# Linear attention and a multiplicative FFN on one core: attention matmuls at full height, another phi, a chunk per batch, and a new order

## The chip, the core and the metric

The kernel runs on one NeuronCore of a Trainium2 chip. Five engines work side by side, each through its own list of instructions in order, and wait for one another by semaphores: TensorE (PE, matmuls, with its weight loads as PEld), VectorE (DVE), ScalarE (ACT), GpSimd (POOL) and SyncE (SP, which only issues DMAs here). Sixteen DMA engines move data; SP, POOL and ACT put work on their queues. PE writes to PSUM (8 banks of 512 fp32 columns), the others read it from there; POOL has no work on PSUM in this kernel.

The metric is the device time of one execution in microseconds. The kernel before took 261.28 us (median of 3 runs, 260.99 to 262.19).

## The reference

```python
def phi(x):                                       # elu(x) + 1
    return np.where(x > 0, x, np.exp(x) - 1.0) + 1.0
q_p, k_p = phi(q), phi(k)                         # q, k, v: 8 batches, 8 heads, 576 tokens, 64
kv  = np.einsum('bhsd,bhse->bhde', k_p, v)        # 64 x 64 for each head
z   = np.sum(k_p, axis=2)
num = np.einsum('bhsd,bhde->bhse', q_p, kv)
den = np.einsum('bhsd,bhd->bhs', q_p, z)[..., None] + 1e-06
x   = (num / den).transpose(0, 2, 1, 3).reshape(4608, 512)
a, b = x @ w1, x @ w2                             # 512 -> 1024
out = ((a * b) @ w3) @ w_out                      # 1024 -> 1024 -> 512
```

All inputs and the output are fp32. Both kernels compute with bf16 operands and fp32 sums, and multiply w3 and w_out once, into one 1024 x 512 matrix wf, so that the last two products become one.

## The kernel before

**Tiles.** The 576 tokens of a batch are four tiles of 128 ("J": token 4p + j is in tile j at partition p) and a rest of 64 ("R"). Two batches share one R tile, one in each half of the partitions. So 36 tiles of 128 tokens stand in `xt` (x transposed, 512 features as four blocks of 128 partitions), in the order: the J tiles of an even batch, the J tiles of the next, their common R tile. A chunk is four tiles in that order, 512 tokens; there are nine, and a chunk can hold tiles of two batches.

**A batch.** k, q and v are loaded as fp32 (1 MB each, the R rows as small DMAs of their own). `phi_exp` (ScalarE, L137) writes exp(x) as bf16, `phi_min` (VectorE, L141) takes min(exp x, 1), and `phi_max` (VectorE, L162) takes max(x + 1, that), one instruction of 256 columns per head. v is cast to bf16 (`v_unit`) into `vt` and `vr`, with a 65th column of ones per head, so that the same matmul gives kv and z.

`kv_half` (L181) multiplies k' by v for two heads at a time (128 x 130). It splits the 128 tokens of a tile into two row halves of 64 and sums each half in a PSUM bank of its own; an R tile uses one half only. ScalarE copies one bank (`kvf`, L203) and VectorE adds the other (L204). q' is transposed by TensorE (`q_tr`, L309, batches 0 to 3) or by a DMA (`qt_load`, L242). `nat_units` (L244) multiplies each head's q' (64 rows) by its kv (64 x 65): eight matmuls of 64 rows for a tile, the two heads of a pair in different banks. VectorE adds 1e-6 to the denominators, takes the reciprocal and multiplies (L271, L273, L275), for two tiles at once where it has two. The result is transposed into `xt` by TensorE (`xt_tr`, L285, batches 1 and 3 here) or a DMA (`xt_load`, L296).

Batch 0 goes another way (`first_kvz`, `first_nd`, `first_rest`): kv and z are masked into 128 x 128 blocks and multiplied with transposed q', so that the result is already transposed; the reciprocal is exp(-ln(den)) on ScalarE.

**The FFN.** `f_unit` (L379) does 128 of the 1024 columns of a and b for a chunk: eight matmuls of 512 columns (L371), a copy of a by ScalarE (L376) and the product by VectorE (L377) into `ab`. `o_unit` (L386) does eight matmuls with wf for a tile (L390), and ScalarE or VectorE copies the result (L393). `o_store` writes each tile by a DMA, `o_last` the last one in two column halves.

**Weights.** POOL issues the loads of w1, w2, w3 and w_out, which cast to bf16. w3 is transposed by TensorE (`w3_tr`, L454) and multiplied with w_out (`wf_mm`, L464).

**Order.** The list `ORDER` is written out by hand: each word is a step (L, M, N load k, q, v; x, X and y, Y and z, Z the three steps of phi for k and q; K kv, A nd, F and O the FFN, S a store, T and D the DMA transposes, P and a the TensorE ones, w, U and W the making of wf, E, C and B loads of w3, w_out and w1/w2; the numbers are batch or chunk, and part). The steps' instructions go to their engines in just this order; a "+" gives a copy to VectorE, or a small load to POOL. `GATES` makes some loads wait for others to land. PSUM: four banks (`mm_ps`) for a, b, o, wf and the transposes of x, two buffers of two banks (`at_ps`) for kv, nd and the other transposes.

Of the kernel before, what the change touches and what calls it, by code (L numbers as in the profile page):

```python
# [14 lines left out]
NCH = 512  # L15


@with_exitstack
def kernel(
# [14 lines left out]
    NTOK = B * S  # L34
# [7 lines left out]
    n_chunks = NTOK // NCH  # L42

    tile_of, order = {}, []
    for b in range(0, B, 2):
        for key in [("J", b, j) for j in range(NJ)] + [("J", b + 1, j) for j in range(NJ)] + [("R", b, 0)]:
            tile_of[key] = len(order)
            order.append(key)  # L50
        tile_of["R", b + 1, 0] = tile_of["R", b, 0]
    NT = len(order)
# [3 lines left out]
    ld = ctx.enter_context(tc.tile_pool(name="ld", bufs=5))  # L56
    ldr = ctx.enter_context(tc.tile_pool(name="ldr", bufs=8))
    setup = ctx.enter_context(tc.tile_pool(name="setup", bufs=2))
# [3 lines left out]
    lr = ctx.enter_context(tc.tile_pool(name="lr", bufs=2))  # L62
    ab_p = ctx.enter_context(tc.tile_pool(name="ab", bufs=2))
    sm = ctx.enter_context(tc.tile_pool(name="sm", bufs=3))
    mm_ps = ctx.enter_context(tc.tile_pool(name="mm_ps", bufs=4, space=bass.MemoryType.PSUM))
    at_ps = ctx.enter_context(tc.tile_pool(name="at_ps", bufs=2, space=bass.MemoryType.PSUM))


    ident = consts.tile([P, P], BF16)
    mask = consts.tile([P, 2, 2, D], BF16)  # L70
    eps = consts.tile([P, 1], F32)
    zero = consts.tile([P, NCH], BF16)

    w1_sb = wpool.tile([P, KC, DFF], BF16)
    w2_sb = wpool.tile([P, KC, DFF], BF16)
    wo_sb = wpool.tile([P, FC, DM], BF16)
    wf_sb = wpool.tile([P, FC, DM], BF16)
    xt = wpool.tile([P, NT, KC, P], BF16)
    vt = wpool.tile([P, NJ, H, D + 1], BF16)
    vr = wpool.tile([P, H // 2, D + 1], BF16)  # L80

    def constants(part):
        if part == 0:
            make_identity(nc, ident)
        elif part == 1:

            nc.gpsimd.memset(mask, 0.0)
            nc.gpsimd.memset(mask[0:D, :, 0, :], 1.0)
            nc.gpsimd.memset(mask[D:P, :, 1, :], 1.0)
            nc.gpsimd.memset(eps, 1e-6)  # L90
            nc.gpsimd.memset(vt[:, :, :, D:D + 1], 1.0)
            nc.gpsimd.memset(vr[:, :, D:D + 1], 1.0)
        else:
            nc.vector.memset(zero, 0.0)

    def warm_up(n):

        ps = mm_ps.tile([P, NCH], F32, tag="mm", name="warm")
        for _ in range(n):
            nc.tensor.matmul(ps, zero[:, 0:P], zero, start=True, stop=True)  # L100


    raw = {}

    def load_qkv(name, src, b, part, alt=False):


        if part == 3:
            t = raw[name + "r", b] = ldr.tile([P, RW], F32, tag="ldr", name=f"{name}32r")
            for hh in range(2):  # L110
                (nc.gpsimd if alt else nc.sync).dma_start(  # L111
                    out=t[hh * R:(hh + 1) * R].rearrange("p (h d) -> p h d", d=D),
                    in_=src[b, hh * 4:(hh + 1) * 4, NJ * P:S, :].rearrange("h p d -> p h d"))
            return None
        if (name, b) not in raw:
            raw[name, b] = ld.tile([P, JW], F32, tag="ld", name=f"{name}32")
        t = raw[name, b]
        h0, h1 = ((0, 4), (4, 8), (0, 8))[part]
        W = NJ * D
        return nc.sync.dma_start(  # L120
            out=t[:, h0 * W:h1 * W].rearrange("p (h x) -> p h x", x=W),
            in_=src[b, h0:h1, 0:NJ * P, :].rearrange("h (p j) d -> p h (j d)", j=NJ))


    ph = {}

    es = {}

    def phi_exp(name, b, g):

        if g == 2:
            x, e = raw[name + "r", b], e_p.tile([P, RW], BF16, tag="er", name="er")
        else:
            x = raw[name, b][:, g * (JW // 2):(g + 1) * (JW // 2)]
            e = e_p.tile([P, JW // 2], BF16, tag="e", name="e", bufs=4)
        es[name, b, g] = x, e
        nc.scalar.activation(out=e, in_=x, func=AF.Exp)  # L137

    def phi_min(name, b, g):
        e = es[name, b, g][1]  # L140
        nc.vector.tensor_scalar_min(out=e, in0=e, scalar1=1.0)  # L141

    def phi_max(name, b, hp):

        if (name, b) not in ph:
            ph[name, b] = [None, None]
        if hp == KC:
            dr = ph[name, b][1] = phi_p.tile([P, RW], BF16, tag=name + "r", name=name + "r", bufs=3)
            todo = [(dr, *es[name, b, 2])]
        else:  # L150
            if hp == 0:
                ph[name, b][0] = phi_p.tile([P, KC, NJ, 2, D], BF16, tag=name + "j", name=name + "j")
            dj = ph[name, b][0]
            x, e = es[name, b, hp // 2]
            W = NJ * D
            todo = []
            for u in range(2):
                h = 2 * (hp % 2) + u
                todo.append((dj[:, hp, :, u, :], *(t[:, h * W:(h + 1) * W].rearrange(
                    "p (j d) -> p j d", d=D) for t in (x, e))))  # L160
        for out, x, e in todo:
            nc.vector.scalar_tensor_tensor(  # L162
                out=out, in0=x, scalar=1.0, in1=e, op0=ALU.add, op1=ALU.max)

    def copy_of(alt):
        return nc.vector.tensor_copy if alt else nc.scalar.copy

    def v_unit(b, i, alt=False):

        if i < 2:  # L170
            copy_of(alt)(  # L171
                out=vt[:, :, 4 * i:4 * i + 4, 0:D],
                in_=raw["v", b].rearrange("p (h j d) -> p j h d", h=H, j=NJ)[
                    :, :, 4 * i:4 * i + 4])
        else:
            copy_of(alt)(out=vr[:, :, 0:D], in_=raw["vr", b].rearrange("p (h d) -> p h d", d=D))


    kvs, qts, xns = {}, {}, {}

    def kv_half(b, g):  # L181


        kj, kr = ph["k", b]
        if g == 0:
            kvs[b] = att.tile([P, KC, 2, D + 1], BF16, tag="kv", name="kv")
        kvp = at_ps.tile([P, 2, 512], F32, tag="at", name="kvp")
        W = 2 * (D + 1)
        for i in range(2):
            hp = 2 * g + i  # L190
            steps = [(kj[:, hp, j].rearrange("p u d -> p (u d)"),
                      vt[:, j, 2 * hp:2 * hp + 2, :].rearrange("p h e -> p (h e)"), (0, 1))
                     for j in range(NJ)]
            steps.append((kr[:, i * P:(i + 1) * P],
                          vr[:, 2 * i:2 * i + 2, :].rearrange("p h e -> p (h e)"), (g,)))
            for n, (kk, vv, halves) in enumerate(steps):
                for r in halves:
                    rows = slice(r * R, (r + 1) * R)
                    nc.tensor.matmul(  # L199
                        kvp[:, r, i * W:(i + 1) * W], kk[rows], vv[rows],  # L200
                        start=(n == 0), stop=(n == (NJ if r == g else NJ - 1)))
        kvf = lr.tile([P, 2 * W], F32, tag="kvf", name="kvf")
        nc.scalar.copy(out=kvf, in_=kvp[:, 0, 0:2 * W])  # L203
        nc.vector.tensor_tensor(  # L204
            out=kvs[b][:, 2 * g:2 * g + 2].rearrange("p a u e -> p (a u e)"), in0=kvf,
            in1=kvp[:, 1, 0:2 * W], op=ALU.add)

    def kv_full(b, g):

        kj, kr = ph["k", b]  # L210
        if g == 0:
            kvs[b] = att.tile([P, KC, 2, D + 1], BF16, tag="kv", name="kv")
        kvp = at_ps.tile([P, 2, 512], F32, tag="at", name="kvp")
        W = 2 * (D + 1)
        rows = slice(g * R, (g + 1) * R)
        for i in range(2):
            hp = 2 * g + i
            for j in range(NJ):
                nc.tensor.matmul(kvp[:, 0, i * W:(i + 1) * W],
                                 kj[:, hp, j].rearrange("p u d -> p (u d)"),  # L220
                                 vt[:, j, 2 * hp:2 * hp + 2, :].rearrange("p h e -> p (h e)"),
                                 start=(j == 0), stop=False)
            nc.tensor.matmul(kvp[:, 0, i * W:(i + 1) * W], kr[rows, i * P:(i + 1) * P],
                             vr[rows, 2 * i:2 * i + 2, :].rearrange("p h e -> p (h e)"),
                             start=False, stop=True)
        return kvp[:, 0, 0:2 * W]

    def kv_copy(b, g, p, alt=False):
        copy_of(alt)(out=kvs[b][:, 2 * g:2 * g + 2].rearrange("p a u e -> p (a u e)"), in_=p)

# [400 lines left out]
```

## Time and profile before

| | |
|---|---|
| median of 3 runs | 261.28 us (260.99 to 262.19) |
| profiled execution: span from first to last instruction | 258.1 us |
| the profiled execution's own device time | not given beside its span |
| mean granted TensorE clock | 0.999 |
| busy: PE / DVE / ACT / POOL | 237.4 / 167.9 / 129.0 / 21.1 us |
| PE busy in 0 to 24.8 us, and in 24.8 to 60 us | 9.13 of 24.8, 34.67 of 35.2 |
| DVE busy in 60 to 110 us | 45.49 of 50 |
| DMA: moved; queue of SP and queue of POOL | 48.98 MB; 61.4% and 14.1% of 16 engines' span |
| HBM read, written | 38.80 MB, 9.44 MB |

How to read it. The span is from the first to the last instruction. "Busy" is the time in which an engine had an instruction; matmuls are pipelined, and the duration of one (380 ns for 512 columns) is longer than the distance to the next, so for TensorE the distance between starts is the price. The "chain" goes back from the last instruction to what released each step. A group's line gives the source line, engine, operation, output and inputs with their shapes, the count, busy us and mean ns of one, and the idle time before with what ended it. "DMA share" is in sixteenths of the DMA engines, and can exceed 1, since an engine's packets overlap.

### The profile page before, as it was taken

What the parts mean: (1) busy time and instruction counts of PE and PEld (TensorE: products, weight loads), DVE (VectorE), ACT (ScalarE), POOL (GpSimd) and SP (SyncE); (2) the same over time, 40 slices, a digit from 0 to 9 for tenths busy, and PEclk for the clock granted to TensorE, in tenths of its full rate; (3) what the DMA queues carried; (4) which work ended last, traced back from release to release, by engine and by line L of the source; (5) the groups of instructions that cost most, each with busy time, mean ns of one, the idle gap of its engine ahead of it and who ended that gap; (6) DMA issues with size and microseconds to landing.
All of it is one profiled execution on the core that took longest, in us unless ns stands there. A gap on an engine that the chain in (4) does not pass through costs nothing.

```text
span 258.1 us, 4507 instructions
## 1 busy us (share of the span) xinstructions
PE 237.4 (92%) x1656; PEld 116.2 (45%) x1673; DVE 167.9 (65%) x426; ACT 129.0 (50%) x205; POOL 21.1 (8%) x42
## 2 busy tenths in 40 slices
PE   1138999999999999999999999999999999999994
PEld 1124554545454454455444444444444444444442
DVE  0025787969978979997968589468866543423320
ACT  2048587858478664677353645726533203331421
POOL 8000765000101000000000000000000000000000
PEclk9999999999999999999999999999999999999999
DMA  6999999999898599939988975934980124003024
GB/s 100 200 257 378 316 229 245 208 334 307 302 291 250 87 340 215 307 104 253 211 193 245 369 160 123 248 99 131 218 220 26 34 57 124 0 37 125 3 82 163
DMA packets 70085, 48.98 MB, mean 190 GB/s; under 512 B 34416, under 2 KB 64368, under 8 KB 70064
## 3 DMA queue, kind: packets, MB, share of 16 engines
q1 hardware_dynamic: 63104, 42.54, 61.4%
q0 software_dynamic: 6816, 6.03, 14.1%
q8 instruction: 13, 0.21, 0.3%
q10 hardware_dynamic: 144, 0.13, 0.1%
q14 instruction: 8, 0.07, 0.1%
HBM read 38.80 MB, written 9.44 MB: 187 GB/s over the span
## 4 chain that ended last, share of the span: by engine, by line
PE 84%; DMA 8%; ACT 2%; SPq 1%; issue 1%; DVE 1%; DVEq 0%; POOLq 0%
PE a_ps L371 25%; PE b_ps L371 24%; PE o_ps L390 23%; DMA k<-in_k_dram 4%; DMA w3b<-in_moe_w_dram 4%; PE kvp L199 3%; PE wf_ps L464 3%; PE nd L265 3%; SPq L111 1%; PE tp L309 1%; PE w3p L454 1%; PE xtp L285 1%; PE o_ps L417 1%; DVE qj L162 1%; ACT e L137 0%
## 5 line engine op out<-in xcount | busy, mean ns | idle before, releaser
L371 PEld LDWEIGHTS <-w_sb 128*128 128x128 bf16 x576 | 54.2, 98 | 63.4 <-issue 0.5
L377 DVE TENSOR_TENSOR ab<-a_sb,b_ps 128x512 bf16<-128x512 f32 x72 | 49.0, 684 | 46.6 <-PE b_ps L371 35.4
L371 PE MATMUL a_ps<-xt,w_sb 128*128 128x512 bf16 x288 | 75.1, 380 | 0.1
L371 PE MATMUL b_ps<-xt,w_sb 128*128 128x512 bf16 x288 | 74.9, 379 | 0.0
L376 ACT COPY a_sb<-a_ps 128x512 f32<-128x512 f32 x72 | 41.9, 586 | 56.8 <-PE a_ps L371 55.6
L390 PE MATMUL o_ps<-wf_sb,ab 128*128 128x512 bf16 x266 | 63.2, 379 | 0.7
L390 PEld LDWEIGHTS <-ab 128*128 128x128 bf16 x280 | 26.7, 98 | 30.8
L393 ACT COPY o_sb<-o_ps 128x512 f32<-128x512 f32 x24 | 14.0, 583 | 30.7 <-PE o_ps L390 30.7
L162 DVE SCALAR_TENSOR_TENSOR kj<-k,e 128x256 bf16<-128x256 f32 x64 | 23.6, 417 | 0.1
L162 DVE SCALAR_TENSOR_TENSOR qj<-q,e 128x256 bf16<-128x256 f32 x64 | 23.4, 417 | 0.1
L141 DVE TENSOR_SCALAR e<-e 128x1024 bf16<-128x1024 bf16 x32 | 13.4, 420 | 14.2 <-ACT e L137 14.2
L137 ACT ACTIVATE e<-q 128x1024 bf16<-128x1024 f32 x16 | 16.7, 1058 | 9.3 <-DMA q<-in_q_dram 9.1
L454 PE MATMUL w3p<-ident,w3b 128*128 128x128 bf16 x64 | 6.1, 253 | 15.0 <-ACT w3t L455 8.0
L137 ACT ACTIVATE e<-k 128x1024 bf16<-128x1024 f32 x16 | 16.9, 1056 | 4.1 <-DMA k<-in_k_dram 2.7
L275 DVE TENSOR_TENSOR xn<-nd,r 128x512 bf16<-128x512 f32 x28 | 18.0, 686 | 0.0
L464 PE MATMUL wf_ps<-wo_sb,w3t 128*128 128x512 bf16 x61 | 16.7, 412 | 1.0 <-ACT w3t L455 0.8
L454 PEld LDWEIGHTS <-w3b 128*128 128x128 bf16 x64 | 4.9, 113 | 16.6 <-DMA w3b<-in_moe_w_dram 8.2
L393 DVE COPY o_sb<-o_ps 128x512 f32<-128x512 f32 x11 | 7.6, 688 | 6.4 <-PE o_ps L390 6.4
L171 ACT CAST vt<-v 128x1024 bf16<-128x1024 f32 x9 | 9.3, 1046 | 2.0 <-DMA v<-in_v_dram 2.0
L203 ACT COPY kvf<-kvp 128x260 f32<-128x260 f32 x14 | 5.3, 375 | 8.9 <-PE kvp L199 8.7
L464 PEld LDWEIGHTS <-w3t 128*128 128x128 bf16 x64 | 6.2, 104 | 7.8 <-issue 1.7
L199 PE MATMUL kvp<-vt,kj 64*128 64x130 bf16 x224 | 9.2, 217 | 0.0
(81 smaller groups left out, 163.5 us busy)
## 6 DMA issues: line engine op xcount, KB each, us to landing
out_dram<-o_sb SPq DMA_DIRECT2D x31, 256.0 KB, 3.2
k<-in_k_dram SPq DMA_DIRECT2D x7, 1024.0 KB, 8.6
q<-in_q_dram SPq DMA_DIRECT2D x7, 1024.0 KB, 8.2
v<-in_v_dram SPq DMA_DIRECT2D x6, 1024.0 KB, 7.4
w3b<-in_moe_w_dram POOLq DMA_DIRECT2D x8, 256.0 KB, 7.1
v<-in_v_dram SPq DMA_DIRECT2D x4, 512.0 KB, 8.5
w_sb<-in_moe_w_dram POOLq DMA_DIRECT2D x8, 256.0 KB, 11.3
out_dram<-o_sb SPq DMA_DIRECT2D x9, 128.0 KB, 2.4
```

The costliest lines, as they stand in the source:

```text
L137: nc.scalar.activation(out=e, in_=x, func=AF.Exp)
L141: nc.vector.tensor_scalar_min(out=e, in0=e, scalar1=1.0)
L162: nc.vector.scalar_tensor_tensor(out=out, in0=x, scalar=1.0, in1=e, op0=ALU.add, op1=ALU.max)
L199: nc.tensor.matmul(kvp[:, r, i * W:(i + 1) * W], kk[rows], vv[rows], start=(n == 0), stop=(n == (NJ if r == g else NJ - 1)))
L275: nc.vector.tensor_tensor(out=dst.rearrange("p (c u) e -> p u c e", u=2), in0=v4[:, :, :, 0:D], in1=r[0:n].unsqueeze(3).to_broadcast([n, 2 ...
L371: nc.tensor.matmul(ps, w[:, kc, f * P:(f + 1) * P], xt[:, 4 * c:4 * c + 4, kc, :], start=(kc == 0), stop=(kc == KC - 1))
L376: nc.scalar.copy(out=a_sb, in_=a_ps)
L377: nc.vector.tensor_mul(out=abs_[c][:, f, :], in0=a_sb, in1=b_ps)
L390: nc.tensor.matmul(o_ps, ab[:, f, m * P:(m + 1) * P], wf_sb[:, f, :], start=(f == 0), stop=(f == FC - 1))
L393: copy_of(alt)(out=o_sb, in_=o_ps)
L454: nc.tensor.transpose(tp[:, kc, :], raw["w3", i][:, kc * P:(kc + 1) * P], ident)
L464: nc.tensor.matmul(wfs[i], w3ts[i][:, kc, :], wo_sb[:, kc, :], start=(kc == 0), stop=(kc == FC - 1))
```

## The change

The kernel function is nearly rewritten.

- **kv at full height** (`kv_full`). All sixteen J matmuls of a batch have 128 rows. The R tile of k is multiplied with a `vr` of 260 columns that holds v of the heads of either half on its diagonal and zeros elsewhere, at 128 rows too. Two copies of 64 partitions put kv on the diagonal of a tile `kv` that was zeroed at the start, for each pair of heads.
- **nd at full height** (`nat`). One matmul of 128 rows and 130 columns gives both heads of a pair, four for a tile in place of eight. Every tile has its own add, reciprocal and product. Batch 0 goes the same way as the others; `first_*`, `mask`, `eps` and the nine warm-up matmuls go.
- **phi** is min(exp x, max(x, 0) + 1): a max-add from the fp32 input (VectorE, or POOL with "+") and a min of two bf16 tiles (VectorE). The R rows of k and q stand in one tile and are done together.
- **A chunk per batch.** Chunk b is the four J tiles of batch b, and chunk 8 all the R rows (`xtr`). `xt` has three buffers.
- **Stores** take two tiles each (512 KB); the loads of k, q and v are halves of a batch, of four heads each.
- **Copies** can also go to POOL ("++"). POOL also casts some of v.
- **PSUM.** `mm_ps` (four banks) is for a, b and wf. O and the transposes have two banks of their own, one for each parity; kv and nd share one buffer of two banks.
- **Order and gates** are new. TensorE begins with the transposes of q of batch 0; w3 and wf come between the steps of batch 0. In the new order TensorE transposes q for batches 0 and 1, and x for batches 0 and 1; a DMA does the others.

The new source also has functions for products from sums of blocks (`g_unit`, `w_unit` and theirs); no word of the new order calls them.

```diff
-    ld = ctx.enter_context(tc.tile_pool(name="ld", bufs=5))
-    ldr = ctx.enter_context(tc.tile_pool(name="ldr", bufs=8))
+    ld = ctx.enter_context(tc.tile_pool(name="ld", bufs=10))
+    ldr = ctx.enter_context(tc.tile_pool(name="ldr", bufs=2))
...
+    xt_p = ctx.enter_context(tc.tile_pool(name="xt", bufs=3))
...
-    at_ps = ctx.enter_context(tc.tile_pool(name="at_ps", bufs=2, space=bass.MemoryType.PSUM))
+    o_ps_p = ctx.enter_context(tc.tile_pool(name="o_ps", bufs=1, space=bass.MemoryType.PSUM))
+    at_ps = ctx.enter_context(tc.tile_pool(name="at_ps", bufs=1, space=bass.MemoryType.PSUM))
...
+    def phi_max1(name, b, g, alt):
+        x, w, r = part_of(name, b, g)
+        y = es["y", name, b, g] = e_p.tile([P, w], BF16, tag="y" + r, name="y" + r, bufs=2)
+        (nc.gpsimd if alt else nc.vector).tensor_scalar(
+            out=y, in0=x, scalar1=0.0, scalar2=1.0, op0=ALU.max, op1=ALU.add)
+
+    def phi_min(name, b, g):
...
+        for c in range(2):
+            nc.vector.tensor_tensor(out=p[0][:, 2 * g + c].rearrange("p j u d -> p u j d"),
+                                    in0=e[:, c], in1=y[:, c], op=ALU.min)
...
+    def kv_full(b, alt):
+        kj, kr = ph["k", b]
+        vt, vr, kv = vts[b % 2], vrs[b % 2], kvs[b % 2]
+        kvp = at_ps.tile([P, 2, NCH], F32, tag="at", name="kvp")
+        W = 2 * E1
+        for i in range(2):
+            for g in range(2):
+                hp = 2 * g + i
+                for j in range(NJ):
+                    nc.tensor.matmul(kvp[:, i, g * W:(g + 1) * W],
+                                     kj[:, hp, j].rearrange("p u d -> p (u d)"),
+                                     vt[:, j, 2 * hp:2 * hp + 2, :].rearrange("p h e -> p (h e)"),
+                                     start=(g == 0 and j == 0), stop=False, skip_group_check=True)
+            nc.tensor.matmul(kvp[:, i, 0:2 * W], kr[:, i * P:(i + 1) * P],
+                             vr[:, i].rearrange("p g u e -> p (g u e)"),
+                             start=False, stop=True, skip_group_check=True)
+        for u in range(2):
+            rows = slice(u * D, (u + 1) * D)
+            copy_of(alt)(out=kv[rows, :, :, u], in_=kvp[rows, :, 0:2 * W].rearrange(
+                "p i (g u e) -> p i g u e", g=2, u=2)[:, :, :, u])
...
+    def nat(b, j):
+        nd = at_ps.tile([P, 2, NCH], F32, tag="at", name="nd")
...
+            nc.tensor.matmul(nd[0:n, g, i * 2 * E1:(i + 1) * 2 * E1], w,
+                             kvs[b % 2][:, i, g].rearrange("p u e -> p (u e)"), start=True, stop=True)
...
+    def o_unit(c, m, alt):
+        ab = abs_[c]
+        o_ps = o_ps_p.tile([P, DM], F32, tag="ou"[m % 2], name="o_ps")
...
+        copy_of(alt)(out=rows_of(c, m // 2)[:, m % 2], in_=o_ps)
...
+    def rows_of(c, r):
+        if (c, r) not in o_sbs:
+            o_sbs[c, r] = sm.tile([P, 2, DM], F32, tag="o_sb", name="o_sb", bufs=2)
+        return o_sbs[c, r]
...
+    L0.0 x0.0 M0.1 R0.0+ y0.0 X0.1 L0.1 x0.2 E2 x0.1 M0.0+ X0.0 N0.1 Y0.1 N0.0+ I1 z0.0 R0.1+
+    v0.0 Z0.1 Y0.0 I0 y0.1 E5 Z0.0 C1 C0 a0.0 v0.1+ v0.2++ z0.1 M1.0 E0 a0.1+ E6 y0.2 w5+ z0.2
+    K0 R1.0+ E3 w2+ A0.3 A0.1 E1 P0.3+ Y1.0 L1.0 B0.0 u2.2 w0 u5.2 M1.1 A0.0 w6 u0.2 w3+ P0.0+
+    B0.1 X1.0 A0.2 N1.0+ u6.2 y1.2 N1.1+ x1.2 w1 X1.1 L1.1 E4 P0.2+ u3.2 Y1.1 z1.2 Z1.1 Z1.0
+    R1.1+ P0.1+ x1.1 u1.2+ y1.0 B2.0 a1.0 E7 h0 B2.1 M2.0 B1.1 x1.0 y1.1 v1.1 v1.0+ a1.1+ T0.1
+    h1 I2 B1.0 z1.1 v1.2 h2 B3.0 z1.0 N2.0 h3 w4+ T1.1 K1+ B3.1 i0 i1 u4.2 A1.2 L2.0 w7 Y2.0+
...
+    K2 Z3.1 L3.1 X3.0 O0.1 R4.0 A2.0 Y3.0 F1.2 A2.3 Z3.0 x3.0 N3.0 y3.2+ x3.2 F1.5 x4.2 M4.0
+    O0.2 N4.1 S0.0 z3.2 T3.0 y3.0+ y3.1 M4.1 T2.1 A2.2 S0.1 v3.0 v3.2++ F1.7 A2.1 x3.1 z3.1 z3.0
+    F1.1 v3.1 F1.4 L4.0 K3+ D2.0 O1.1 Y4.0+ X4.0 Y4.1 A3.0 Z4.0 y4.2 O1.2 A3.2 N4.0 O1.3+ O1.0+
...
+    F7.1 F7.5 S6.0 S6.1 F7.6 D7.1 O7.1+ O7.0 F8.0 F8.3 F8.4 F8.5 O7.2 O7.3 F8.2 S7.0 F8.6 F8.1
+    F8.7 O8.0+ S7.1 O8.1 S8.0 Q8.3 O8.2 H8.2
...
+    GATES = "N0.0<M0.1 L1.0<E6 B0.0<E1 B0.1<E5 L1.1<E0 B1.1<N1.0 B2.0<E0 B3.1<E5 M1.0<C0 M1.1<M1.0 L2.1<L1.0 N2.1<B1.1 M2.0<B2.1 M2.1<M1.0 N3.0<L2.1 L3.1<L0.0 N3.1<E3"
```

(In the new order y and Y are the max-add and z and Z the min; u makes wf, R loads R rows, H stores one tile. In `GATES`, "N0.0<M0.1" lets the load N0.0 start when M0.1 has landed.)

## The prediction

> **What bounds the kernel now.** I read the busy line and the slices of the page first, then the stretches of the span by engine, then the chain that ended last, in order of time, and for prices the groups of instructions.
>
> ```profile
> PE 237.4 (92%) x1656; PEld 116.2 (45%) x1673; DVE 167.9 (65%) x426; ACT 129.0 (50%) x205; POOL 21.1 (8%) x42
> ...
> PE 84%; DMA 8%; ACT 2%; SPq 1%; issue 1%; DVE 1%; DVEq 0%; POOLq 0%
> ```
>
> TensorE carries 84% of the chain. The stretches (columns: window, length, busy time of PE, PEld, DVE, ACT, POOL with counts, clock, DMA share, GB/s) say where it is idle:
>
> ```profile
> 0.00:24.80 24.80, 9.13 (x51) 5.27 (x52) 4.75 (x14) 8.94 (x11) 5.35 (x18) 1.00 1.01 227
> 24.80:60.00 35.20, 34.67 (x279) 18.48 (x280) 28.67 (x72) 26.29 (x40) 13.30 (x20) 1.00 1.23 269
> 60.00:110.00 50.00, 49.84 (x391) 24.86 (x393) 45.49 (x124) 32.11 (x52) 2.45 (x4) 1.00 0.99 263
> ...
> 160.00:200.00 40.00, 39.88 (x291) 18.63 (x292) 27.72 (x73) 19.81 (x34) 0.00 (x0) 1.00 0.61 158
> ...
> 254.40:258.20 3.80, 0.00 (x0) 0.00 (x0) 0.00 (x0) 0.37 (x1) 0.00 (x0) 0.89 0.30 109
> ```
>
> From 24.8 to 254.4 PE is never really idle, though VectorE is at 91% in 60 to 110. So 258.1 us is a start, a dense stretch that is the sum of all matmuls, and a tail of 3.7. Only what shortens one of the three counts, or what opens a hole in the second. The unit prices are in the chain (start, us, work):
>
> ```profile
> 33.32 0.23 PE kvp L219 x4
> ...
> 36.91 0.45 PE w3p L454 x8
> ...
> 37.79 1.73 PE wf_ps L464 x8
> ...
> 75.68 1.13 PE kvp L199 x36
> 76.81 0.97 PE a_ps L371 x4
> 77.78 0.86 PE b_ps L371 x4
> 79.00 0.97 PE a_ps L371 x4
> ```
>
> A 512-column matmul takes 1.73/8 = 0.216 us, a 128-column transpose 0.45/8 = 0.056. Four a_ps matmuls take 0.97 behind kv or nd work and their b_ps twins 0.86: the change from 64-row to 128-row tiles costs 0.11. Between the b_ps that ends at 78.64 and the next a_ps at 79.00 stand sixteen 64-row nd matmuls, 0.36 with the change into them.
>
> **Dense TensorE work.** Before: 229.6 us of stretch, plus what ran earlier at full-speed prices (24 transposes 1.3, 12 wf matmuls 2.6, 8 q transposes 0.45) 4.4, is 234.0. The idle in the start is then 24.8 - 4.4 = 20.4. The change takes out:
> - Nine warm-up matmuls: 9 x 0.216 = 1.9.
> - Half of the TensorE transposes of q (64 to 32, the rest go to DMA): 32 x 0.056 = 1.8. The 32 transposes of xn stay, for batches 0 and 1 in place of 1 and 3.
> - kv. Before: fourteen 64-row halves take 9.1 in all, eleven groups of them are followed by a 0.11, and batch 0 takes 1.8: 12.0. After: eight batches of sixteen 128x130 matmuls and two 128x260 ones. The nearest row is L219 in the chain, four 128x130 in 0.23, 0.057 each: 16 x 0.057 + 2 x 0.11 = 1.13, times eight 9.0. Saved 3.0.
> - nd. Before: 280 matmuls in 21 groups, 6.7 in all, plus 21 x 0.11, plus batch 0 by its own way (eight of 512 columns and eight of 64, 2.0): 10.9. After: 40 tiles of four 128x130 at 0.057: 9.1. Saved 1.9.
>
> F, O, the w3 transposes and wf keep their counts. Sum: 234.0 - 8.6 = 225.4. The R tiles still load 64-column weights; if each of the eight pays one 0.11 it is 226.3. I take 226.
>
> The Trainium skill speaks against this part: TensorEngine Tiling (Array Packing), When to Use Tiling, wants two row tiles for a contraction of 64, which run at once, where the new diagonal multiplies zeros. By that rule alone nd would lose (0.23 for a tile of four, against 0.18 with its change of height, is 40 x 0.05 = 2 us) and nothing would be won; its Key Properties do name the drain at a change of mode, and the 0.97 beside 0.86 is that drain, so here the rows decide for the edit.
>
> **VectorE, ScalarE, POOL: no price, by this cover.** The prices are in the groups (mean ns behind the busy us):
>
> ```profile
> L162 DVE SCALAR_TENSOR_TENSOR kj<-k,e 128x256 bf16<-128x256 f32 x64 | 23.6, 417 | 0.1
> ...
> L275 DVE TENSOR_TENSOR xn<-nd,r 128x512 bf16<-128x512 f32 x28 | 18.0, 686 | 0.0
> L141 DVE TENSOR_SCALAR e<-e 128x1024 bf16<-128x1024 bf16 x32 | 13.4, 420 | 14.2 <-ACT e L137 14.2
> ...
> L171 DVE CAST vt<-v 128x1024 bf16<-128x1024 f32 x7 | 4.8, 702 | 0.0
> ...
> L286 DVE COPY xt<-xtp 128x512 bf16<-128x512 bf16 x3 | 1.2, 416 | 0.0
> ```
>
> phi before: 32 min at 0.42, 128 STT at 0.417 and 10 for the tails are 77 of summed durations (which overlap a little). After: 24 max-adds on VectorE, nearest row the fp32 CAST of 1024 columns at 0.70, 17; five for tails 2; 72 two-source bf16 min of 512 columns. No row shows a bf16 min in SBUF: between 0.416 (the COPY of 512 bf16) and 0.686 (the TENSOR_TENSOR on fp32 from PSUM) I take 0.416, the row of its type: 30. That is -28. The nd evictions go from 35 to 40 of 0.16 + 0.18 + 0.69, +5, the first batch's own products go, -5, and copies that move between engines come to nearly nothing: about -27, and -8 with 0.686. VectorE kept PE dense before with more, so either way it costs nothing by its load. ScalarE loses the kvf copies and the Ln/Exp pairs. POOL gets eight max-adds of 1024 columns, three of 512 and some v casts; its memsets of 128 and 256 columns took 0.22 and 0.36, which makes 1.2 for 1024, and I keep twice that, 2.4, as the upper end. POOL does nothing in 110 to 200, and some 2.2 us of PE work lies between such a step and its min: covered at 1.2; what it costs beyond is rival 3.
>
> The Trainium skill, GPSIMD Engine Reference, Engine selection, would leave elementwise work on VectorE, and its Key points say that the two share SBUF interfaces; no run shows it. By that rule, with VectorE held 1.2 in each of the eleven steps, 13 of the 27 come back, and the sum is the same.
>
> **New waits.** kv and nd now share one buffer of two banks (two buffers before), so each of 39 kv and nd steps waits on PE until the step before is evicted: 1.03 of VectorE, or the ScalarE copies. All F and O matmuls are queued behind a waiting nd. Most have an F or O (1.73) between, which covers 1.03 plus 0.7 of VectorE queue. Walked through batch 2 with row durations, the evictions end 0.1 to 1.5 us before the next step needs the bank. I take 1.5 in all, 0 to 8. O has two banks of its own, F four: looser than before.
>
> **Start.** Before, the first wf waited for w3, and eight of them took 3.62 at the cold clock against 1.73. Now PE's first work is q's transposes. q's first half is issued on POOL behind four tail loads (0.65 each) and a w3 block, at about 5, and lands 4 (first w3b) to 10 us (median of half loads) later; exp 1.06, min, two transposes and copies, kv at about 17, nd, its eviction (1.0, twice, PE waiting), first wf at about 22.6. By then 3.6 of dense work is done: idle 19.0, and part of the cold 1.7 on top: I take 20. Bounds: wo must have landed. The same mix of bytes was in by 24.7 before (DMA share 1.01), at the later 1.23 it would be 20: idle 16.4 to 22.8. The gates hold w1 and w2 behind w3. Before, all weights and two batches were in at 55.6; now two to four half loads of batch 2 (1.6 each over 16 engines, 1.3 at that share) stand ahead of the last w block, +3 to +5, but the first large load goes out at 0.7 and not at 5.0, -4: 54 to 57. Its F has 37 of dense work ahead, so comes at 57: hidden, barely, and rival 2 if not.
>
> **DMA and queues.** Loads are halves (four on POOL, the rest on SP); SP issues 12 large transposes for 9 and 16 small for 15, and 16 stores of 512 KB and the tails in place of 40 smaller ones. Large ones took 4.3 us from issue to landing (204.20 to 208.46). A batch is needed at its own chunk, not 9/8 of it, so up to 15 us nearer the end; the share of 0.61 at 160 to 200 covers it. As before, a DMA waits for the eighth ahead of it on its queue. Priced nothing; without that cover each late xt transpose costs up to 4.3.
>
> **Tail.** Before: the last o_ps ends at 254.35, half a copy 0.37, a store from 254.81, end at 258.1: 3.75. After: the last unit is a whole copy (0.58) and two SP issues (0.56 each): +0.2 +0.6, and twice the bytes, +0.4: 5.0.
>
> **Sum.** 20 + 226 + 1.5 + 5.0 = 252.5, against 20.4 + 234.0 + 3.7 = 258.1, the span of the profiled execution, the only time given of it. The median of the runs shown is 261.28, 3.2 above, and I add that for what lies around the span: 255.7.
>
> **Rivals.**
> 1. The single bank pair costs more: 0.2 at each of 39 steps is 8 for 1.5, time 262.2, no change. For: VectorE at 91% in 60 to 110. Against: it loses 8 to 27 of its work. Chance 0.07.
> 2. The start is 3 later by the order of loads (idle 23): 258.7, still faster. For: the DMA share of 1.01 at once. Against: the early first loads. 0.13.
> 3. Slower: POOL. A max-add or cast on POOL is awaited by a min on VectorE, behind which F's products queue in order, and behind those PE, for banks. Over 2.7 us in place of 1.2 (cover 2.2) eleven steps cost 0.5 each, 5.6 in all, and the gain is gone; at 3.5 it is 14, 269. For: no row of POOL arithmetic. Against: the memset rows. 0.17.
> 4. Full height doesn't save: if a 128x130 matmul takes 0.078 (the 0.23 over three gaps), 288 of them cost 6 more: 262. Against: the chain's 0.33 for the next four holds the change of height, not a slower pace. 0.02.
> 5. Better: no waits and idle 17: 251.2. 0.12.
>
> **Chances and range.** The forecast, 253 to 258, has the other 0.49. 0.5%, 1.3 us, is about what can be told from no change. Faster: 0.49 + 0.12 + 0.13 = 0.74; same: rivals 1 and 4, 0.09; slower: rival 3, 0.17. The range goes from 250.5, just under rival 5, to 263, past rivals 1 and 4; the longer POOL cases and a still earlier start, under 0.2, are left out.
>
> **What would show it.** Right: PE over 99% busy from about 25 to 249, a_ps at 0.86 behind kv and nd, kv at 1.13 a batch, the first wf before 23, VectorE under 155. Wrong: PE idle before nd, ended by VectorE (1); before wf or early F, ended by a load (2); POOL rows over 2.7 (3); kv over 1.5 a batch (4). A start idle past 23 or holes of more than 5 make the prediction wrong.

## The result

The changed kernel takes 268.31 us (median of 4 runs, 267.70 to 270.69) against 261.13 (260.53 to 262.19): a ratio of 1.028 (95% interval 1.023 to 1.034), 7.2 us slower. The forecast was 255.7. The profiled execution has a span of 266.0 us and a device time of 267.82. The ratios below are each against runs of the kernel before on the same chip, and compare undisturbed runs only, so that one can stand a little beside the ratio of the medians.

The busy line and the shares of the chain, of the page after:

```profile
PE 234.5 (88%) x1368; PEld 118.2 (44%) x1368; DVE 157.5 (59%) x339; ACT 114.7 (43%) x172; POOL 67.8 (25%) x69
...
PE 69%; DMA 19%; SPq 4%; DVE 2%; issue 2%; POOL 1%; ACT 1%; ACTq 0%; DVEq 0%; POOLq 0%
```

TensorE carried 84% of the chain before; now transfers and SP's queue have 23% of it (9% before). The stretches (window, length, busy time of PE, PEld, DVE, ACT, POOL with counts, clock, DMA share, GB/s) say where:

```profile
0.00:24.90 24.90, 6.90 (x62) 6.03 (x63) 10.41 (x21) 8.81 (x10) 15.90 (x33) 1.00 1.03 244
24.90:60.00 35.10, 35.10 (x267) 19.89 (x265) 25.88 (x60) 22.14 (x30) 15.55 (x20) 1.00 1.17 260
60.00:110.00 50.00, 47.16 (x268) 22.58 (x267) 38.13 (x86) 25.52 (x38) 18.90 (x9) 1.00 1.04 272
110.00:160.00 50.00, 44.09 (x247) 21.29 (x245) 31.64 (x71) 25.83 (x42) 10.18 (x5) 0.97 0.99 254
160.00:200.00 40.00, 39.88 (x236) 20.00 (x235) 28.24 (x62) 15.00 (x23) 7.25 (x2) 1.00 0.54 116
261.40:266.00 4.60, 0.02 (x1) 0.00 (x0) 0.00 (x0) 0.59 (x1) 0.00 (x0) 0.87 0.42 101
```

TensorE is full from 25 to 60 and from 160 on, and has holes between: 2.8 us idle in 60 to 110 and 5.9 in 110 to 160 by busy time, where the DMA share is about 1 (it was 0.99 and 0.82 in these stretches before). The chain (start, us, work) names what ends them:

```profile
76.72 5.36 DMA v<-in_v_dram
...
82.10 0.02 ACT vt L196
...
83.05 0.59 ACT a_sb L315
...
83.68 1.02 PE a_ps L310 x4
...
89.16 7.34 DMA xt<-xn
...
96.54 1.02 PE a_ps L310 x4
...
100.16 0.23 PE nd L268 x4
100.38 0.86 PE a_ps L310 x4
...
107.52 0.34 PE nd L268 x4
107.86 0.97 PE a_ps L310 x4
...
111.35 3.52 DMA qtr<-kqr
...
114.92 0.64 PE nd L268 x4
115.56 4.81 PE o_ps L467 x16
...
135.87 9.41 DMA qt<-qj
...
145.32 0.40 PE nd L268 x4
```

Two kinds of wait stand out: TensorE itself waits for a transpose (96.5, 114.9, 145.3), or ScalarE stands at the cast of a v that has not landed, and a copy that TensorE needs is queued behind it (83.7, and again at 139.5). The longest wait, at 114.9, is for a small transpose, of q's rest rows. It landed in 3.52 us, near the median of its kind (3.8), so it was not slow but issued late: SP had been issuing without a pause of over 0.5 us since 86. After 3.5 us without a matmul, up to 114.9, sixteen o_ps take 4.81, where they take 3.56 elsewhere: 1.2 more, at a granted clock of 0.50 in 115 to 118 us.

Holes are read as the distance between two matmuls' ends over the unit price. From 24.9 on they sum to 12.0 us; 3.8 of it is the one at 114.9. So the span is: idle start 21.3 + dense work 228.1 + holes 12.0 + tail 4.6 = 266.0, against 20.4 + 234.0 + 0 + 3.7 = 258.1 before. TensorE did lose 5.9 us of work; the holes took 12.0, the start 0.9 and the tail 0.9.

The large transposes in the view of the DMAs (count, median us from issue to landing), of before and then of after:

```profile
xt<-xn SPq DMA_TRANSPOSE x5, 4.6
qt<-qj SPq DMA_TRANSPOSE x4, 4.9
```

```profile
qt<-qj SPq DMA_TRANSPOSE x6, 7.2
xt<-xn SPq DMA_TRANSPOSE x6, 6.2
```

Three large transposes more, and slower by the median. The trace tells how many other large transfers (loads, stores, transposes) were still on their way when each of the twelve was issued:

| large transfers in flight at issue | transposes | us from issue to landing |
|---|---|---|
| 0 | 3 | 4.55, 4.94, 6.28 (the last with six small transfers ahead) |
| 1 | 3 | 4.27, 5.09, 5.92 |
| 2 | 1 | 6.03 |
| 3 | 2 | 7.34, 8.39 |
| 4 | 3 | 8.63, 9.32, 9.41 |

A fitted line has 4.7 us for none and 1.05 for each transfer ahead. Before, one transpose of nine met three (it took 7.86), none four.

A slow transpose also keeps SP itself, which issues in order. With four large transfers ahead, and with none (start, us on SP):

```profile
79.46 6.61 SPq L239 DMA_TRANSPOSE qt<-qj  x1
...
183.57 1.32 SPq L239 DMA_TRANSPOSE qt<-qj  x1
```

The twelve hold SP for 48.3 us in all (the nine before: 24.1). From 60 to 110 SP issues for 45.7 of 50 us (31.8 before), so whatever stands behind a transpose goes out late.

### The profile page after: what moved, and what is told of

Read it like the earlier page. It is cut to its first block, busy times and chain, and to the rows that moved or that the text cites. A ratio compares the mean times of both kernels' runs of the same rounds, so it can differ in the third digit from the quotient of the medians.

```text
span 266.0 us, 3839 instructions
## 1 busy us (share of the span) xinstructions
PE 234.5 (88%) x1368; PEld 118.2 (44%) x1368; DVE 157.5 (59%) x339; ACT 114.7 (43%) x172; POOL 67.8 (25%) x69
## 4 chain that ended last, share of the span: by engine, by line
PE 69%; DMA 19%; SPq 4%; DVE 2%; issue 2%; POOL 1%; ACT 1%; ACTq 0%; DVEq 0%; POOLq 0%
PE a_ps L310 19%; PE o_ps L467 18%; PE b_ps L310 18%; DMA xt<-xn 6%; PE wf_ps L143 5%; DMA q<-in_q_dram 5%; DMA qt<-qj 4%; DMA v<-in_v_dram 3%; PE nd L268 3%; SPq L104 3%; PE kvp L217 2%; PE w3p L136 2%; DMA qtr<-kqr 1%; POOL kq32r L104 1%; PE xtp L289 1%
## 5 line engine op out<-in xcount | busy, mean ns | idle before, releaser
L310 PE MATMUL a_ps<-xt,w_sb 128*128 128x512 bf16 x256 | 66.7, 379 | 2.4 <-ACT a_sb L315 2.0
L173 POOL TENSOR_SCALAR y<-k 128x1024 bf16<-128x1024 f32 x4 | 14.8, 3702 | 45.0 <-DMA k<-in_k_dram 29.9
L173 POOL TENSOR_SCALAR y<-q 128x1024 bf16<-128x1024 f32 x4 | 14.6, 3638 | 36.8 <-DVE r L272 14.7
L268 PE MATMUL nd<-kv,qt 128*128 128x130 bf16 x128 | 12.5, 219 | 3.0 <-DVE xn L274 1.7
L143 PE MATMUL wf_ps<-wt_sb,w3t 128*128 128x512 bf16 x64 | 15.1, 379 | 0.0
L173 DVE TENSOR_SCALAR y<-q 128x1024 bf16<-128x1024 f32 x12 | 8.7, 727 | 10.3 <-DMA q<-in_q_dram 10.3
L190 DVE TENSOR_TENSOR qj<-e,y 128x512 bf16<-128x512 bf16 x32 | 12.0, 418 | 3.9 <-DMA qt<-qj 2.5
L268 PEld LDWEIGHTS <-qt 128*128 128x128 bf16 x128 | 9.4, 98 | 10.7 <-DVE xn L274 3.1
L190 DVE TENSOR_TENSOR kj<-e,y 128x512 bf16<-128x512 bf16 x32 | 13.5, 468 | 0.2 <-POOL y L173 0.2
L173 DVE TENSOR_SCALAR y<-k 128x1024 bf16<-128x1024 f32 x12 | 9.5, 796 | 4.7 <-DMA k<-in_k_dram 4.7
```

The lines of the kernel that those rows point to most:

```text
L143: nc.tensor.matmul(wfs[i], w3ts[i][:, kc, :], wo_sb[:, kc, :], start=(kc == 0), stop=(kc == FC - 1))
L173: (nc.gpsimd if alt else nc.vector).tensor_scalar(out=y, in0=x, scalar1=0.0, scalar2=1.0, op0=ALU.max, op1=ALU.add)
L190: nc.vector.tensor_tensor(out=p[0][:, 2 * g + c].rearrange("p j u d -> p u j d"), in0=e[:, c], in1=y[:, c], op=ALU.min)
L268: nc.tensor.matmul(nd[0:n, g, i * 2 * E1:(i + 1) * 2 * E1], w, kvs[b % 2][:, i, g].rearrange("p u e -> p (u e)"), start=True, stop=True)
L310: nc.tensor.matmul(ps, w[:, kc, f * P:(f + 1) * P], xt_of(c)[:, :, kc, :], start=(kc == 0), stop=(kc == KC - 1))
```

## The theories

A: transfers. Batch b is now wanted at its own chunk, with more transposes; loads of later batches, issued ahead, fill the DMA engines, so transposes and loads land late. B: POOL's max-adds, whose rows are three times my price. C: the one bank pair of kv and nd; the profile of after speaks against it already, since PE waited 1.7 us in all for xn at nd, 1.36 of that in the start. No run tried a second pair.

## Experiments: taking transfers away

Each of these leaves out part of the data, so its output is not the reference's; all matmuls stay.

**No large transposes.** Batches 2 to 7 use the transposed q and x of batch 1.

```diff
 def qt_load(b, part):
     ...
+    if part == 0 and b > 1:
+        qts[b, 0] = qts[1, 0]
+        return
     ...
 def xt_load(b, part):
     if part == 0:
+        xts[b] = xts[1]
+        return
     ...
```

> The changed kernel without the twelve large DMA transposes (q and x of batches 2 to 7): these batches read the transposed q and x of batch 1, so q' and x of batches 2 to 7 are left out of the result, and six times 2 x 512 KB of transposes with their waits are gone. All matmuls stay. Theory A: the holes that end with such a transpose (96.5, 145.3, 166.0) go, and the loads behind them come earlier, so those at 83 to 88 and 115 shrink: 7 to 10 us less, 258 to 261. Theories B and C: kv, nd and their inputs stay as they are, 266 to 269.

259.31 us, ratio 0.993 (0.989 to 0.996): 9.0 less than the changed kernel. Stretches:

```profile
60.00:110.00 50.00, 49.58 (x285) 24.69 (x289) 41.91 (x93) 31.19 (x45) 18.66 (x9) 1.00 0.98 275
110.00:160.00 50.00, 49.25 (x289) 24.84 (x292) 35.56 (x82) 25.52 (x42) 13.88 (x6) 1.00 0.68 201
```

The holes are gone, with POOL at the same work and the bank pair unchanged.

**No large transposes of x** (the second half of that edit).

> The changed kernel without the six large transposes of x (batches 2 to 7 read the transposed x of batch 1, so their x is left out of the result); the six of q stay. Theory A: about half of the 9 us, 262.5 to 265.5, since the holes at 96.5 and 166 ended with a transpose of x, those at 115 and 145 with one of q. If only the transposes of q matter, through the single buffer of q' that VectorE has to wait for: 267 to 269. Theories B and C: 267 to 269.

262.13, ratio 1.004 (1.001 to 1.006): 6.2 less. Two thirds of the 9.0 lie with x, a little more than expected.

**No v of batches 2 to 7.**

```diff
-    ... M2.1 F0.4 ... N2.1 ... v2.1++ R2.1 ... v2.0 ...
+    (no N, v and R .1 of batches 2 to 7; vt and vr keep batch 0's and 1's)
```

> The changed kernel without the loads and casts of v of batches 2 to 7 (6.8 of 28 MB of k, q and v); these batches use the v of batch 0 or 1, so their v is left out of the result. All twelve large transposes and all matmuls stay. Theory A1 (a transpose lands late because loads issued ahead of it, for batches not yet wanted, are still in flight): the transposes land in 4 to 5 us in place of 5 to 9, and most of the 9 us that leaving the transposes out gave comes back: 260 to 264 against 268.3. Theory A2 (twelve large transposes are too many in themselves, whatever else is in flight): 266 to 269. Theories B (POOL) and C (one bank pair): 266.5 to 268.5.

255.97, ratio 0.982 (0.978 to 0.986): 12.3 less, as much as all of the holes and more than either side expected. The twelve transposes are all there:

```profile
60.00:110.00 50.00, 49.68 (x286) 24.71 (x289) 41.38 (x91) 25.49 (x39) 15.33 (x5) 1.00 0.88 218
110.00:160.00 50.00, 49.05 (x289) 24.90 (x292) 35.69 (x81) 21.50 (x35) 13.07 (x4) 1.00 0.89 208
```

```profile
qt<-qj SPq DMA_TRANSPOSE x6, 4.5
xt<-xn SPq DMA_TRANSPOSE x6, 5.6
```

So it is not their number alone (A2), but what else is on the way (A1). With v go also its casts and 24 of SP's issues; the next run keeps the issues.

**A quarter of each v load.** Issues, waits and buffers as they were, three quarters of the bytes of v gone from the large loads; the casts handle the quarter alone too (on ScalarE 0.41 us in place of 1.05).

```diff
+    nh = 1 if name == "v" and b > 1 else 4
...
-        in_=src[name][b, 4 * g:4 * g + 4, 0:NJ * P, :]
+        in_=src[name][b, 4 * g:4 * g + nh, 0:NJ * P, :]
...
```

> The changed kernel where each half load of v of batches 2 to 7 brings one head of its four, and the cast handles that one alone (the v of the other heads of these batches is left out: batch 0's or 1's stands there). Issues, waits of SP and buffers are as in the changed kernel; 4.7 MB of 50.6 are not moved. If the bytes in front of the transposes on the DMA engines make the holes: most of the 12.3 us of the run without v comes back, 257 to 261. If the number of issues on SP or the ring of load buffers makes them: 266 to 268.5.

262.67, ratio 0.998 (0.992 to 1.004), so some 260.8 against its before-runs of 261.4: 5.6 us less by the medians, 8 by the ratios. By either figure the bytes, with the shorter casts, make about half of the holes or more. In its trace (span 261.9) no wait behind a cast of v is left: TensorE waits 2.6 us for a large transpose of q that took 9.3 behind other loads and stores, and 1.1 for a small one. What is left is of the same kind; how it parts between the bytes on the way and SP's time was not separated.

## Experiments: POOL

**All of POOL's arithmetic to VectorE, where it stood.** `y2.2+` becomes `y2.2`, and so on for eleven max-adds; the v casts marked `++` become `+`.

> The changed kernel with every max-add and v cast of POOL given to VectorE (eleven max-adds of about 0.75 us, five small v copies). Theory A (transfers: a large transpose or load is issued late on SP or lands late, and TensorE waits for it): the 12.4 us of holes in TensorE stay, 267 to 270 against 268.3 of the changed kernel. Theory B (the 3.7-us max-adds of POOL, and their effect on VectorE, make k', q' and so kv and nd late): 260 to 264. Theory C (kv and nd share one pair of banks): VectorE has 8 us more work, so slightly slower, 268 to 271.

274.70, ratio 1.054 (1.047 to 1.061): slower than any side said. Its waits:

```profile
DVE y L173 <- DMA q<-in_q_dram: 12.8, 4, 5.7
...
PE nd L268 <- DVE xn L274: 10.7, 5, 5.9
```

VectorE now stands at an early max-add until its load lands (up to 5.7 us), and nd's eviction behind it, and behind that PE. This run does not price POOL.

**The same, each max-add directly before its min** (and the v casts on ScalarE).

```diff
-    ... Y4.0+ X4.0 Y4.1 A3.0 Z4.0 ...
+    ... X4.0 Y4.1 A3.0 Y4.0 Z4.0 ...
```

> The changed kernel with no arithmetic on POOL, and each of its eleven max-adds put on VectorE directly before the min that reads it, so that VectorE, unlike in the first run without POOL's arithmetic, does not stand in front of a load early (its five v casts go to ScalarE). Theory B (POOL's 3.7 us make k' and q' late): 261 to 265. Theory A: the holes stay, VectorE has 8 us more work with room for it, 267 to 271.

268.07, ratio 1.027 (1.022 to 1.033): the same as the changed kernel, with no max-add on POOL and TensorE busy as in the changed kernel (46.94 of 50 us in 60 to 110, 44.18 in 110 to 160). Theory B falls: POOL's steps are long, but without them the time is the same. The groups, of after and then of this run:

```profile
L173 POOL TENSOR_SCALAR y<-k 128x1024 bf16<-128x1024 f32 x4 | 14.8, 3702 | 45.0 <-DMA k<-in_k_dram 29.9
...
L190 DVE TENSOR_TENSOR qj<-e,y 128x512 bf16<-128x512 bf16 x32 | 12.0, 418 | 3.9 <-DMA qt<-qj 2.5
...
L190 DVE TENSOR_TENSOR kj<-e,y 128x512 bf16<-128x512 bf16 x32 | 13.5, 468 | 0.2 <-POOL y L173 0.2
```

```profile
L190 DVE TENSOR_TENSOR kj<-e,y 128x512 bf16<-128x512 bf16 x32 | 11.9, 416 | 0.2
```

A max-add of 1024 columns takes POOL 3.7 us, and min on VectorE waits 0.2 for it in all. The min of k has a mean of 468 ns with POOL at work and 416 without, 1.6 us over the kernel. Four of its 32 rows make all of that: two of 0.62 us beside casts on POOL, and one of 1.26 and one of 0.82 that began within 0.1 us of a max-add on POOL. Five mins that ran wholly inside a max-add took 0.41 to 0.43. The Trainium skill (GPSIMD Engine Reference, Key points) has POOL and VectorE share SBUF interfaces, and collide where VectorE has two inputs in SBUF: the four rows agree, the five do not.

## Experiments: SP's queue

**Small loads on POOL**, first on the run without POOL's arithmetic, then on the one with late max-adds. `R2.0` becomes `R2.0+`, to `R7.1+`.

> As the kernel without POOL's arithmetic, and the 36 small loads of the R rows of batches 2 to 7 are issued by POOL in place of SP (0.6 us each on SP, 22 us in all). Theory A, if the time that SP spends on issuing is what makes transfers late: 4 to 6 us below the kernel without POOL's arithmetic. Theory A, if the DMA engines themselves are full (share 0.91 to 1.08 in 60 to 160 us): within 1.5 us of it. Theories B and C: the same as it.

272.72, ratio 1.045 (1.039 to 1.050), against 1.054 of its base: 2 us less, with overlapping intervals.

> The kernel with the max-adds on VectorE directly before their mins (268.07), and the 36 small loads of the R rows of batches 2 to 7 issued by POOL in place of SP: 22 us of SP's time free, the same bytes. If SP's time for issuing makes the holes: 261 to 264. If the bytes do: 266.5 to 269.

268.02, ratio 1.023 (1.017 to 1.030), against 1.027 of its base: no difference beyond the intervals. SP issues for 33.0 of 50 us from 60 to 110 in place of 42.6 in the base, so SP's time alone is not what is short. Its trace has the wait for the small transpose at 1.0 us, but a new one of 5.0, until 67.9, for a copy queued behind the cast of a v that landed at 66.3.

**All loads of batches 2 to 7 on POOL** (`L`, `M`, `N`, `R` with a `+`).

> As the kernel without POOL's arithmetic, and all loads of k, q and v of batches 2 to 7, large and small, are issued by POOL, so that SP's queue holds transposes and stores alone. Theory A, if transposes are late because they stand behind loads in SP's one queue (7 to 9 us from issue to landing): 6 to 9 us below the kernel without POOL's arithmetic. Theory A, if the DMA engines are full whatever the queue: within 2 us of it. Theories B and C: the same as it.

310.93, ratio 1.192 (1.187 to 1.197): 36 us worse than its base, where 6 to 9 better was expected of a free SP queue. From its chain:

```profile
76.26 14.32 DMA qt<-qj
...
102.57 26.15 DMA xt<-xn
...
163.84 23.18 DMA qt<-qj
```

With a queue to themselves, the seven large transposes that have POOL's loads beside them take 6.5 to 26 us, the three above the longest, and the five at the end, where none do, 4.3 to 5.6. The Trainium skill (DMA: Bandwidth & Descriptors, Queues, rings and completion order) has each DMA engine take the packets of its queues in turns: a queue of its own is not precedence, and these rows agree.

**Other orders.** First only loads are moved: those within 25 steps ahead of a large transpose, where no step between reads them, come directly after it (18 loads, some past two transposes).

```diff
-    ... R3.0 M3.1 ... R2.1 ... N3.1 ... M3.0 T2.0 L3.0 ...
+    ... T2.0 R3.0 M3.1 R2.1 N3.1 M3.0 L3.0 ...
```

> The changed kernel with another order of the loads alone: of the loads that stood within 25 steps ahead of a large transpose, those that no step between reads are issued directly after it (23 moves). Theory A1, if the place in SP's queue decides: with one large transfer fewer ahead of a transpose it lands about 1.05 us sooner (the slope over the twelve large transposes of the changed kernel: 4.7 us with none in flight, 8.6 to 9.4 with four), and holes of 3 to 6 us go: 262 to 266. If the loads so held back then come late for exp, kv and the chunk: 268 to 272. Theory C: 267 to 270.

292.34, ratio 1.118 (1.109 to 1.128). The transposes are quick, by the issues, and the loads late, by the waits:

```profile
qt<-qj SPq DMA_TRANSPOSE x6, 4.8
xt<-xn SPq DMA_TRANSPOSE x6, 4.8
```

```profile
POOL y L173 <- DMA q<-in_q_dram: 49.4, 3, 21.5
...
POOL y L173 <- DMA k<-in_k_dram: 40.5, 2, 32.6
```

SP stands at a transpose until q' or x is made, and the loads behind it with it. The DMA share falls to 0.70 in 60 to 110: transfer time is thrown away, and TensorE is busy for 37.56 of 50 us there.

Then the loads and phi of later batches were delayed, by 8 steps more for each batch; by 20 alike; and by 8 together with the loads moved behind transposes, as above.

```diff
-    ... v2.1++ R2.1 z2.0 F0.6 Y2.1 N3.1 x2.1 v2.0 ...
+    (L, M, N, R, x, X, y, Y, z, Z, v of batch b moved back, at most to just before their readers)
```

> The changed kernel with another order and nothing else: the loads of k, q and v, their exp, max-add, min and casts come later in the order, by up to 8 steps for batch 3, 16 for batch 4, up to 40 for batch 7, where their readers (kv and the transposes of q) allow it. All work is kept. Theory A1 (transposes stand behind loads that are issued too far ahead): the DMA share in 60 to 160 us falls below 0.95, the transposes of batches 4 to 7 land in 4.3 to 7 us, and 3 to 7 us come back: 261 to 265 against 268.3. If no room was to be had (loads then land too late for exp and kv): 267 to 275. Theory C: no change, 267 to 270.

> As the spread order, but every batch from 2 on has these steps later by up to 20 places alike, so that as many loads are in flight, only later. Theory A1: not better than the changed kernel where batches 2 and 3 already had no room: 267 to 273, and worse than the spread order. Theory C: 267 to 270.

> The spread order, and then the loads within 25 steps ahead of a large transpose issued after it. Theory A1: the two add up, 258 to 263. If loads are now too late: 266 to 275. Theory C: 267 to 270.

304.21 (1.167), 321.81 (1.231) and 326.11 (1.248). In the first, TensorE waits 22.0 us for two casts of v, up to 15.0 for one, behind a late load. All three went far beyond what was expected: the order has no slack on the side of the loads either.

## Experiments: buffers, and less transposing by DMA

**More buffers**: `ld` with 16 in place of 10; and 14, with two for `kj` and `qj`.

> The changed kernel with sixteen buffers for the half loads in place of ten, nothing else. If SP waits in order for a load buffer, and the transposes behind it with it, and this makes the rest of the holes: 262 to 265 against 268.3. If the bytes ahead of the transposes make them, loads run further ahead and nothing is won: 267 to 272.

> The changed kernel with fourteen buffers for the half loads and two buffers in place of one for q' and k' of the J tiles. If VectorE's wait for the transpose that still reads q' (2.5 us at qj, and what queues behind it) makes the rest: 2 us or more below the run with sixteen buffers. If not: within 1.5 us of it.

269.08 (1.029, 1.021 to 1.036) and 268.55 (1.029, 1.022 to 1.037): no difference. Neither the number of load buffers nor VectorE's wait for q' is the limit.

**q of batches 2 and 3 transposed by TensorE**: `T2.0` becomes `a2.0 a2.1+`, `T3.0` likewise.

> The changed kernel with q of batches 2 and 3 transposed by TensorE (two times sixteen transposes, 1.8 us of TensorE, and copies on ScalarE and VectorE) in place of two large DMA transposes at 65 and 79 us. All work is kept. If transfers in the stretch from 60 to 160 us make the holes: 3 to 5 us of holes less for 1.8 of work, 264.5 to 267. If two transposes fewer change nothing later: 269 to 271.

267.92, ratio 1.023 (1.017 to 1.029). In its trace, of an execution 2.2 us under its median, the holes after 25 us sum to 7.7 in place of 12.0, and 1.8 of work is added; its span is 263.9. By the ratios 1.5 us come back, within the intervals: two fewer transposes help about as much as they cost.

> Both of the two edits before: small loads on POOL, no arithmetic there, q of batches 2 and 3 transposed by TensorE. All work is kept. If both bear on the same holes: 262 to 266; by bytes alone 264.5 to 267; if neither does: 268 to 271.

271.47, ratio 1.037 (1.032 to 1.043): together they are worse. TensorE now waits 4.5 us at 72.6 for a q' that it has to transpose, as it waited for a copy in the run with small loads on POOL: each edit moves the waits elsewhere.

## Experiment: full height alone, in the kernel before

kv and nd of batches 1 to 7, with the zeroed diagonals, all else as before.

```diff
...
-                for u in range(2):
-                    rows = slice(u * D, (u + 1) * D)
-                    nc.tensor.matmul(nd[0:n, u, hp * (D + 1):(hp + 1) * (D + 1)], w[rows],
-                                     kvs[b][rows, hp, u, :], start=True, stop=True)
+                g, i = divmod(hp, 2)
+                nc.tensor.matmul(nd[0:n, g, i * 2 * (D + 1):(i + 1) * 2 * (D + 1)], w,
+                                 kvs[b][:, hp].rearrange("p u e -> p (u e)"), start=True, stop=True)
...
```

> The kernel before with one part of the change alone: kv and nd of batches 1 to 7 at full height on a zeroed diagonal, in the old order, with the old phi, the old two buffers of two banks and the old chunks. By the prices of the prediction kv saves 10.3 - 7 x 1.13 = 2.4 us and nd 9.0 - 35 x 0.23 = 1.0, all on a TensorE that has no holes: 3.4 us less, 257 to 258 against 260.8. If this part itself brings waits (the copies on the diagonal, the product of one tile after another): 260 to 263.

262.38, ratio 1.004 (1.002 to 1.006): 1.3 slower, not 3.4 faster. From the first a_ps of chunk 1 to the last matmul it takes 185.8 us (before: 186.2). By sums of the distances between matmuls in that part, for six batches:

| | before | full height |
|---|---|---|
| kv | 7.42 | 6.91 |
| nd | 5.72 | 8.23 |
| a_ps over the price of b_ps (changes of height) | 2.3 | 0.2 |

The changes of height went, 2.1, and kv gained 0.5, but nd costs 2.5 more. 6.9 of the 8.23 is thirty tiles at 0.23, as priced; 0.5 is a wait for VectorE; 0.8 is the R tiles, whose 64-column weights cost a change before and behind. Its chain:

```profile
70.27 0.35 PE nd L269 x4
70.62 0.97 PE a_ps L375 x4
```

What it loses lies earlier: chunk 1 begins at 70.55 in place of 68.16, with 2.1 of waits for the cast of v before batch 1's kv; why that v is cast later was not tried.

## Why the prediction was wrong

**The step that failed** is "DMA and queues: priced nothing". The sum has 1.5 us of holes, meant for the bank pair; 12.0 came, and they are 10.5 of the 13.5 us by which the span of 266.0 exceeds the 252.5 of the sum (the start 1.3, the dense work 2.1, the tail -0.4). The bound I gave myself was holes of more than 5. I had the sentence "without that cover each late xt transpose costs up to 4.3" and named as cover the DMA share of 0.61 at 160 to 200, since a batch would be needed "up to 15 us nearer the end". The runs show it needed earlier. Without v or without the large transposes, where few holes are left, kv of batch 3 starts at 85.3 to 85.6 us (97.9 before), of batch 7 at 179.3 to 179.4 (193.1 before), of every batch from 2 on 4 to 14 us sooner. So nine of the twelve large transposes, and four of the six of x, are issued before 165 us, in a stretch whose share was 0.82 to 0.99 before already.

The price was wrong too. The 4.3 from issue to landing came from a single transpose at 204 us with nothing ahead of it; the same trace has one of 7.9 at 180, with three large transfers ahead, and in the full stretch of the changed kernel they took 5 to 9.4. Leaving out transposes gives back 9.0, leaving out v 12.3 with every transpose kept, three quarters of v's bytes 5.6 to 8. That transfers make the holes is shown by this; how much of it is the DMA engines' load and how much SP's one queue, which slow transposes hold, stays open.

**Start.** 21.3 of idle for 20, within its bounds; the first wf at 24.93, not 22.6. The half of q landed at 13.76, inside the range given; then casts of v, min of k and the copy of transposed q take turns on VectorE, 1.36 of wait for an eviction stands before the second nd, as expected of the bank pair. Rival 2's 3 us did not come: the start was 1.3 later, and w1 and w2 were not late.

**Dense work.** 228.1 for 226. kv took 0.45 + 0.11 + 0.46 + 0.12 = 1.14 a batch (1.13 priced), nd 0.23 a tile, a_ps behind it 0.86: the rows held. Of the 2.1, the R tiles pay a change on both sides (0.34, then 0.97), 1.8 in place of the upper 0.9. The run in the kernel before shows that the saving of full height was over-read: for kv and nd I had 4.9, 3.4 of it for batches 1 to 7, and over six batches 0.4 came (0.1 by the rows of the table), 0.5 more without its wait for VectorE. The 5.9 us that the changed kernel did save come mostly from elsewhere: the warm-up, the transposes of q and batch 0's own way. This split is worked out and was not tested part by part.

**The bank pair (rival 1)** cost 0.3 us past the start, by the profile; it was not the limit.

**POOL (rival 3).** Its condition, rows over 2.7 us, came true at 3.7, three times the price taken from memsets, and its consequence did not: with no max-add on POOL the time is the same. That its 269 (for rows of 3.5) stands beside the measured 268.3 is luck: the mechanism was another.

**VectorE.** 157.5 busy for "under 155". The min took 0.42 us in 60 of 64 rows, the lower bound.

**Tail.** 4.6 for 5.0. **Around the span** lay 1.8 us in the profiled execution; I had added 3.2, the distance from one span to a median.

## What to carry to other kernels

A DMA's time from issue to landing is not a property of the DMA: take it from the stretch in which it will be issued, with the transfers that will stand before it, and treat a DMA share near 1 as a bound even while TensorE is still full. A saving on the bounding engine pulls the demand of every transfer earlier, so price the transfers against the shortened time, and say which way each moves. A price from another operation on the same engine (a memset for a max-add) needs a wide bound, and a cheaper form of one product should be counted in the whole sequence, its odd tiles included.

## What the runs showed that I had not expected

- A large transpose took 4.3 to 4.9 us from issue with nothing ahead, about 1.05 more for each large transfer in flight (fitted over twelve), and up to 26 when another engine's queue was loading beside it. It held SP's queue for 1.3 to 3.1 us with no large transfer ahead, for 5.2 to 6.6 with four.
- Moving 18 loads behind transposes they had stood in front of cost 24 us, and giving VectorE early max-adds 6: an in-order engine or queue that reaches a wait early holds up everything behind it.
- A max-add of 128 x 1024 fp32 to bf16 took POOL 3.70 us, where a memset of 256 columns was 0.36.
- One wait of 3.5 us was followed by six matmuls at about twice their price, 1.2 us in all; the granted clock was 0.50 in 115 to 118 us.
